# Two steps of a conversion queue behind each of the first four blocks of the last stage, instead of behind two of them

## The chip, the cores and the metric

The kernel runs on one core of a Trainium2 chip. The metric is the device time of one execution in microseconds (us). Inputs are fp32 arrays; 1.6 us (0.3%) and more can be told from no change with this kernel's spread.

## What is computed

Three layers, one behind the other, for a batch of 2, 768 positions and 512 channels (8 heads of 64). The last one, in which the change lies, is shortened here from the reference:

```python
x = attention(q, k, v, n_global, n_local)      # banded, with a bias by distance
xt = x.transpose(0, 2, 1)                      # token mixing, then channel mixing
u = x + (np.maximum(xt @ w_tok1, 0.0) @ w_tok2).transpose(0, 2, 1)
x = u + np.maximum(u @ w_ch1, 0.0) @ w_ch2
theta = x @ w_theta                            # the rotation layer
zr, zi = x * np.cos(theta), x * np.sin(theta)
y = np.einsum('ts,bsd->btd', w_tok_r, zr) + np.einsum('ts,bsd->btd', w_tok_i, zi)
u = x + y
out = u + np.maximum(u @ w_ch, 0.0)
```

## The kernel before

**Arithmetic.** Every product is made of three matmuls of split operands: a value is kept as a high and a low part, and `mm3` (L71) adds high x high, high x low and low x high. So all weights and activations have to be split before TensorE can read them.

**The conversion queue.** The weights arrive as 64-bit words in 512 KB pieces. Each piece is a job with four phases, and `tick` (L162) moves every running job one phase on, issues the loads of the next jobs (two ahead, into three raw buffers, on the queue of SP) and starts one more job. The phases are `job_scale` (two instructions on ScalarE, L120 and L121), `job_join` (two on VectorE, L126 and L129, and one on GpSimd, L130), `job_high` (one on ScalarE, L138) and `job_low` (one on VectorE, L141). A full step thus issues 3 instructions on ScalarE, 3 on VectorE and 1 on GpSimd, for four jobs. `need(job)` (L178) runs steps, one behind the other, until that job is through its four phases.

**The rotation stage.** `PhaseB.run` (L1051) goes through 12 blocks, (batch, 128 positions), numbered 0 to 11 here. The order in which a block's work is written out is the order of each engine's queue, since the scheduler is switched to manual. For block i:

- `mix(i, 0)`: 24 matmuls of `y` from the rotated values `z` and three pieces of `w_tok` (`wri`), over 256 columns;
- `rotate(i + 1)`: VectorE multiplies `x` with sine and cosine (L954), ScalarE copies the high part (L955), GpSimd subtracts for the low part (L957) and puts `x` together again (L961). `z` has two buffers;
- `turn(i + 3)`: four transposes of `x` into PSUM (`xt_..p`), split by ScalarE (L588) and VectorE (L594);
- `theta(i + 2)`: 12 matmuls of `th`, five instructions of VectorE (L923 to L931) and three of ScalarE (L934 to L936, the sines);
- `mix(i, 1)`, and in blocks 7 to 11 `last`: 24 matmuls of `v` from `u` and the four pieces of `w_ch` (`wch`). `last` calls `need(wch_job)` first (L1022), and `last_split` (L1003), called in blocks 6, 8 and 10, prepares `u` on ScalarE and VectorE (L1016, L1017);
- one step of the queue (L1069), `mix(i, 2)`, and a second step where L1071 asks for it (L1072).

`turn`, `theta` and `last` share two PSUM buffers (`wps`) in turn. In the last block of a batch VectorE also adds `y` to `x` (L995, L999). When block 0 starts, `w_tok`'s pieces 11 to 13 are in the queue's phases; the rest of `w_tok` (to piece 17) and the four pieces of `w_ch` (`wch0` to `wch3`) follow.

Of the kernel before, what the change touches and what calls it, by code (L numbers as in the profile page):

```python
# [875 lines left out]
class PhaseB:  # L876
# [174 lines left out]
    def run(self):  # L1051
        K = self.k
        n = len(self.todo)
        ends = [(b, c, half) for b in range(B) for c in (2, 0, 1) for half in ((0, 1), (2, 3))]
        ends[-1:] = [(1, 1, (2,)), (1, 1, (3,))]
        for i, (b, s) in enumerate(self.todo):
            self.mix(i, 0)
            if i + 1 < n:
                self.rotate(i + 1)
            if i + 3 < n:  # L1060
                self.turn(i + 3)
            if i + 2 < n:
                self.theta(i + 2)
            if b == 1 and s in (0, 2, 4):
                self.last_split(*ends[s][0:2])
            self.mix(i, 1)
            if b == 1 and s > 0:
                self.last(*ends[s - 1])
            K.tick()  # L1069
            self.mix(i, 2)  # L1070
            if i in (0, 2):  # L1071
                K.tick()  # L1072
        self.last_split(*ends[6][0:2])
        self.last(*ends[5])
        for j in range(6, len(ends)):
            if j in (6, 8):
                self.last_split(*ends[j + 2][0:2])
            self.last(*ends[j])
# [54 lines left out]
```

## Time and profile before

| | us |
|---|---|
| median of 3 runs | 522.35 |
| lowest, highest | 521.91, 523.35 |
| the profiled execution | 523.1 |
| its span in the trace | 521.0 |
| TensorE busy (matmuls) | 503.8 |
| VectorE, ScalarE, GpSimd busy | 302.9, 238.5, 167.5 |

All times of rows are from one profiled execution, in us from the start of its span. PE is TensorE's matmuls, PEld its weight loads, DVE VectorE, ACT ScalarE, POOL GpSimd and SP the engine that issues the DMAs. A row of a timeline holds instructions of one kind that follow each other, with their count; `[x <-y]` at its end is idle time of the engine before it and what ended that. The granted clock is a share of full speed: 1.00 is TensorE's level of 2.4 GHz, 0.50 that of 1.2 GHz. The rotation stage starts at 342 us and goes to the end; its blocks 0 to 6 take 11.6 to 11.7 us each.

### The profile page before, as it was taken

Reading aid. Unit: us, or ns where it says so; the run is one execution under the profiler, and the core shown is the slowest. Engines: PE = TensorE matmul, PEld = TensorE weight load, DVE = VectorE, ACT = ScalarE, POOL = GpSimd, SP = SyncE. Lnnn points to the kernel's source line nnn. Section 1 sums busy time; section 2 is a strip of 40 time slices with the busy share of each in tenths; the row PEclk is TensorE's granted clock in tenths of the full one; section 3 lists DMA queues with packets and bytes.
Section 4 is the critical chain, followed back from the end, with each engine's and each line's share of the span. In section 5 each row is a group of like instructions: output and inputs, shape, how many; then the busy total and the mean of one; then the engine's idle time right before and its main releaser. Section 6 shows DMA issues by size and latency. Waiting matters only on the chain.

```text
span 521.0 us, 7902 instructions
## 1 busy us (share of the span) xinstructions
PE 503.8 (97%) x2994; PEld 442.1 (85%) x2994; DVE 302.9 (58%) x676; ACT 238.5 (46%) x463; POOL 167.5 (32%) x175
## 2 busy tenths in 40 slices
PE   7999999999899999999999999999999996999997
PEld 3888878787889999998989889888888885889997
DVE  4667775269975661116473664578785864433252
ACT  4888887347765441112554535325554432133010
POOL 6645454133342320001331152235454433223000
PEclk9999999899999999999999999999999998999999
DMA  7977546135453430002442122212120000000012
GB/s 224 280 203 190 160 125 178 46 122 155 128 161 122 129 115 0 1 0 70 121 135 81 42 81 62 84 59 82 40 82 1 1 0 1 20 21 20 21 62 101
DMA packets 30620, 45.93 MB, mean 88 GB/s; under 512 B 1904, under 2 KB 22384, under 8 KB 30576
## 3 DMA queue, kind: packets, MB, share of 16 engines
q1 hardware_dynamic: 30576, 45.36, 29.0%
q8 instruction: 25, 0.41, 0.3%
q14 instruction: 19, 0.16, 0.1%
HBM read 42.21 MB, written 3.15 MB: 87 GB/s over the span
## 4 chain that ended last, share of the span: by engine, by line
PE 80%; DVE 10%; ACT 3%; DMA 2%; POOL 1%; issue 1%; POOLq 0%; SPq 0%; DVEq 0%; ACTq 0%
PE gp L77 19%; PE h L77 18%; PE y L77 17%; PE v L77 7%; PE th L77 6%; PE o L350 4%; PE t L426 3%; PE mm L77 3%; PE s L383 2%; DVE cvs L126 1%; DVE x L803 1%; POOL base L273 1%; DMA a<-v 1%; DVE cvt L129 1%; ACT e L405 1%
## 5 line engine op out<-in xcount | busy, mean ns | idle before, releaser
L130 POOL TENSOR_TENSOR cvt<-cvt,cvs 128x512 int32<-128x512 int32 (+1 forms) x57 | 76.4, 1340 | 221.2 <-DVE cvt L129 214.0
L77 PE MATMUL gp<-xh,wc 128*128 128x384 f32 x384 | 103.7, 340 | 1.9 <-DVE xl L594 1.6
L77 PE MATMUL h<-wc,g 128*128 128x512 f32 x432 | 102.5, 391 | 0.0
L77 PEld LDWEIGHTS h<-wc,g 128*128 128x128 f32 x432 | 80.6, 188 | 15.8
L590 DVE SCALAR_TENSOR_TENSOR g<-gp,g 128x384 fp32r<-128x384 f32 x48 | 26.7, 557 | 93.3 <-ACT g L588 93.1
L77 PEld LDWEIGHTS gp<-xh,wc 128*128 128x128 f32 x384 | 69.9, 188 | 3.3 <-DVE xl L594 1.8
L77 PE MATMUL gp<-xl,wc 128*128 128x384 f32 x192 | 64.6, 337 | 0.0
L588 ACT ACTIVATE g<-gp 128x384 fp32r<-128x384 f32 x48 | 23.5, 490 | 80.5 <-PE gp L77 80.5
L77 PE MATMUL y<-wri,z 128*128 128x256 f32 (+1 forms) x288 | 53.9, 342 | 0.0
L77 PE MATMUL y<-wri,s 128*128 128x256 f32 (+1 forms) x288 | 52.8, 338 | 0.0
L77 PEld LDWEIGHTS y<-wri,z 128*128 128x128 f32 x288 | 45.5, 191 | 6.9
L426 PE MATMUL t<-ident,e 128*128 128x128 f32 x176 | 48.0, 285 | 3.2 <-ACT at L433 3.1
L77 PEld LDWEIGHTS y<-wri,s 128*128 128x128 f32 x288 | 44.8, 188 | 6.7
L405 ACT ACTIVATE e<-e,mn 128x256 f32<-128x256 f32 (+1 forms) x96 | 39.3, 482 | 17.6 <-DVE mn L395 17.6
L126 DVE SCALAR_TENSOR_TENSOR cvs<-cvt,cvs 128x512 int32<-128x512 int32 (+1 forms) x57 | 43.9, 770 | 0.1
L426 PEld LDWEIGHTS t<-ident,e 128*128 128x128 f32 x176 | 31.7, 185 | 11.3 <-ACT at L433 11.0
L120 ACT ACTIVATE cvt<-raw 128x512 f32<-128x512 f32 (+1 forms) x57 | 37.4, 656 | 2.2 <-issue 2.2
L121 ACT ACTIVATE cvs<-raw 128x512 int32<-128x512 uint16 (+1 forms) x57 | 37.5, 658 | 0.0
L77 PEld LDWEIGHTS gp<-xl,wc 128*128 128x128 f32 x192 | 36.1, 188 | 0.9
L395 DVE CUSTOM_DVE_ANT_0 e<-s,base 128x256 f32<-128x256 f32 (+1 forms) x96 | 32.8, 395 | 5.5 <-PE warm L284 2.3
L934 ACT ACTIVATE w<-w 128x512 f32<-128x512 f32 x12 | 7.6, 632 | 61.1 <-DVE w L931 61.1
L350 PE MATMUL o<-v,at 128*128 128x65 f32 x192 | 32.3, 252 | 0.0
(132 smaller groups left out, 799.7 us busy)
## 6 DMA issues: line engine op xcount, KB each, us to landing
raw<-w_ch SPq DMA_DIRECT2D x28, 512.0 KB, 3.5
raw<-w_tok SPq DMA_DIRECT2D x21, 512.0 KB, 3.5
k<-k SPq DMA_DIRECT2D x8, 480.0 KB, 4.2
q<-q SPq DMA_DIRECT2D x8, 384.0 KB, 3.1
v<-v SPq DMA_DIRECT2D x8, 384.0 KB, 4.5
out<-o SPq DMA_DIRECT2D x11, 256.0 KB, 2.1
raw<-w_theta SPq DMA_DIRECT2D x4, 512.0 KB, 3.6
a<-v SPq DMA_DIRECT2D x8, 240.0 KB, 5.2
```

Of the source, the lines that this page charges most:

```text
L77: self.nc.tensor.matmul(out, lhsT=a, rhs=b, start=first and i == 0, stop=last and i == n - 1)
L120: nc.scalar.activation(out=f(t), in_=f(top), func=AF.Copy, scale=2.0**-111)
L121: nc.scalar.activation(out=s, in_=nxt, func=AF.Copy, scale=2.0**-13)
L126: nc.vector.scalar_tensor_tensor(out=s, in0=t, scalar=-(1 << 31), in1=s, op0=ALU.bitwise_and, op1=ALU.bitwise_or)
L130: nc.gpsimd.tensor_tensor(out=t, in0=t, in1=s, op=ALU.add)
L350: self.nc.tensor.matmul(po[:, j * OW : j * OW + D + 1], lhsT=at, rhs=v[:, j * (D + 1) : (j + 1) * (D + 1)], start=first, stop=last,)
L383: nc.tensor.matmul(ps[j][:, ii, c0:], lhsT=t["q"][pj, i * P : (i + 1) * P], rhs=kf[pj, i * KW - P + c0 : i * KW + P], start=True, stop=True,)
L395: nc.vector.tensor_tensor_reduce(out=e, in0=ps[j][:, ii, c0:], in1=self.base[2 * hp + j][min(i, 1)], op0=ALU.add, op1=ALU.min, scale=-SCAL ...
L405: nc.scalar.activation(out=e, in_=e, func=AF.Exp, bias=mn[:, ii, j : j + 1], scale=-1.0,)
L426: nc.tensor.transpose(pt[:, ii, c, :], e[j][:, ii, c * P : (c + 1) * P], self.ident)
L588: nc.scalar.activation(out=hi, in_=ps, func=AF.Relu if relu else AF.Copy)
L590: nc.vector.scalar_tensor_tensor(out=lo, in0=ps, scalar=0.0, in1=f(hi), op0=ALU.max, op1=ALU.subtract)
```

## The change

```diff
             K.tick()
             self.mix(i, 2)
-            if i in (0, 2):
+            if i < 4:
                 K.tick()
```

Blocks 1 and 3 get a second step of the queue each, behind `mix(i, 2)`. No job, load or instruction is added or dropped; the order of the jobs stays. By the code, the steps and the phases of `w_ch`'s pieces fall as follows:

| block | steps before | `w_ch` before | steps after | `w_ch` after |
|---|---|---|---|---|
| 0 | 2 | | 2 | |
| 1 | 1 | | 2 | |
| 2 | 2 | scale 0 | 2 | scale 0, 1; join 0 |
| 3 | 1 | scale 1; join 0 | 2 | scale 2, 3; join 1, 2; high 0, 1; low 0 |
| 4 | 1 | scale 2; join 1; high 0 | 1 | join 3; high 2; low 1 |
| 5 | 1 | scale 3; join 2; high 1; low 0 | 1 | high 3; low 2 |
| 6 | 1 | join 3; high 2; low 1 | 1 | low 3 |
| 7, `need` in `last` | 2 | high 3; low 2, 3 | 0 | |
| 7 to 11 | 1 each | (empty steps) | 1 each | (empty steps) |

## Rows read from the trace of the kernel before

**Rows 1.** Page, section 2: TensorE's busy tenths and clock, 40 slices of 13 us

```profile
PE   7999999999899999999999999999999996999997
...
PEclk9999999899999999999999999999999998999999
```

**Rows 2.** TensorE's waits, 300 to 521 us: total us, times, longest us

```profile
PE v L77 <- DVE wch L141: 3.2, 1, 3.2
PE v L77 <- ACT wch L138: 1.5, 1, 1.5
```

**Rows 3.** Timeline, TensorE, from 428: start, length, line, operation, out<-in, [idle before]

```profile
432.75 1.11 PE L77 MATMUL v<-u,wch 128*128 128x256 f32 x8
...
446.36 3.01 PE L77 MATMUL y<-wri,s 128*128 128x256 f32 x24
...
455.23 3.04 PE L77 MATMUL v<-u,wch 128*128 128x256 f32 x24
458.11 2.95 PE L77 MATMUL y<-wri,s 128*128 128x512 f32 x12
460.89 3.02 PE L77 MATMUL y<-wri,z 128*128 128x256 f32 x24
```

**Rows 4.** Stretches: length; PE, PEld, DVE, ACT, POOL busy; clock; DMA; GB/s

```profile
353.91:365.56 11.65, 11.65 (x66) 10.05 (x65) 10.10 (x13) 5.65 (x11) 6.61 (x5) 1.00 0.31 91
...
438.94:442.61 3.67, 3.67 (x16) 3.45 (x17) 0.67 (x1) 0.00 (x0) 0.00 (x0) 0.50 0.02 4
```

**Rows 5.** Timeline of VectorE in blocks 6 and 7

```profile
425.35 1.23 DVE L1017 TENSOR_TENSOR u<-x,u 128x1024 fp32r<-128x1024 f32 x1 [2.97 <-ACT u L1016]
426.49 0.69 DVE L141 SCALAR_TENSOR_TENSOR wch<-cvt,wch 128x512 fp32r<-128x512 f32 x1
427.09 0.68 DVE L126 SCALAR_TENSOR_TENSOR cvs<-cvt,cvs 128x512 int32<-128x512 int32 x1
...
428.15 2.39 DVE L954 TENSOR_TENSOR w<-x,w 128x512 f32<-128x512 f32 x2
431.81 0.69 DVE L594 TENSOR_TENSOR xt<-xt_4p,xt 128x512 fp32r<-128x512 f32 x1 [1.26 <-POOL s L957]
...
435.95 0.43 DVE L931 TENSOR_SCALAR w<-w 128x512 f32<-128x512 f32 x1
436.29 0.68 DVE L141 SCALAR_TENSOR_TENSOR wch<-cvt,wch 128x512 fp32r<-128x512 f32 x1
438.92 0.69 DVE L141 SCALAR_TENSOR_TENSOR wch<-cvt,wch 128x512 fp32r<-128x512 f32 x1 [1.95 <-ACT wch L138]
```

**Rows 6.** Timeline of ScalarE in block 7

```profile
437.67 0.71 ACT L936 ACTIVATE w<-w,halfpi 128x512 f32<-128x512 f32 x1
438.28 0.61 ACT L138 ACTIVATE wch<-cvt 128x512 fp32r<-128x512 f32 x1
```

**Rows 7.** Timeline of VectorE in blocks 0, 1 and 5

```profile
351.52 0.69 DVE L141 SCALAR_TENSOR_TENSOR wri<-cvt,wri 128x512 fp32r<-128x512 f32 x1
...
356.31 2.38 DVE L954 TENSOR_TENSOR w<-x,w 128x512 f32<-128x512 f32 x2
...
364.46 0.68 DVE L141 SCALAR_TENSOR_TENSOR wri<-cvt,wri 128x512 fp32r<-128x512 f32 x1
...
403.63 0.69 DVE L995 TENSOR_TENSOR x<-y,x 128x512 f32<-128x512 f32 x1 [0.66 <-PE y L77]
404.23 1.28 DVE L954 TENSOR_TENSOR w<-x,w 128x512 f32<-128x512 f32 x2
```

**Rows 8.** Timeline of GpSimd in block 1

```profile
358.10 3.01 POOL L957 TENSOR_TENSOR s<-w,s 128x512 fp32r<-128x512 f32 x2
```

**Rows 9.** Timeline of TensorE: where blocks 5 and 6 start

```profile
400.57 3.01 PE L77 MATMUL y<-wri,z 128*128 128x256 f32 x24
...
412.20 3.01 PE L77 MATMUL y<-wri,s 128*128 128x256 f32 x24
```

**Rows 10.** DMA issues, 335 to 521 us: count, KB, median us to landing

```profile
raw<-w_ch SPq DMA_DIRECT2D x4, 512.0 KB, 3.9
```

## Prediction

> **What bounds the kernel now.** I first read the page's slices: TensorE is busy nine tenths and more nearly everywhere in the rotation stage (342 to 521 us of the span), with one hole in the slice that begins at 430 us, and the clock row dips in that same slice [rows 1]. The waits of TensorE after 300 us then name the hole. Two waits of matmuls on `v` make up almost all of it, 3.2 us on VectorE's `wch` at L141 and 1.5 on ScalarE's `wch` at L138 [rows 2]. Everywhere else in the stage TensorE waits for nobody: in block 1 it is busy 11.65 of 11.65 us at clock 1.00 [rows 4]. So the rotation stage is TensorE's own time plus that one stall, and only the stall can be won.
>
> The stall sits in block 7, at the first call of `last`. By the code, blocks 0 to 6 run 9 steps of the queue, and the fourth piece of `w_ch` needs 11 from there to be finished; so `K.need(K.wch_job)` in block 7 issues the two missing steps back to back, just before the matmuls that read them. On VectorE the low half of `wch2` (436.29) stands behind the five instructions of theta(9), the last of them at 435.95 [rows 5]. On ScalarE the high half of `wch3` (438.28) stands behind the sines of theta(9), the last at 437.67 [rows 6]; its low half follows on VectorE at 438.92 [rows 5]. TensorE's order has nothing else to do meanwhile.
>
> **What the stall costs.** From the start of `v` in block 7 (432.75) to the start of block 8 (446.36) TensorE needs 13.61 us for 24 matmuls of `v` and 12 of `y` [rows 3]. The same two pieces in block 8 take 458.11 - 455.23 = 2.88 and 460.89 - 458.11 = 2.78, together 5.66 [rows 3]. The excess is 13.61 - 5.66 = **7.95 us**. The two waits are 4.7 of that [rows 2]. The other 3.25 are the clock: after the first wait the granted clock goes from 1.00 to 0.50 (the 1.2 GHz level) for 438.94 to 442.61 [rows 4], so the rest of `v` and the `y` behind it run slowly. If the waits go, I expect the clock loss to go with them, because TensorE holds 1.00 through the blocks before [rows 4].
>
> **The change, part by part.** It adds no instruction and no byte, and since a step issues only to ScalarE, VectorE, GpSimd and SP, TensorE's order stays as it was. Two steps move: one more behind block 1, one more behind block 3. Blocks 0 to 6 then run 11 steps, `wch3` is finished in block 6, and the `need` of block 7 finds nothing to do. *Gain*: 7.95 us if nothing else is late.
>
> *Is `wch3` in time?* Its low half is issued where block 6 now has that of `wch1`, at 426.49 [rows 5]; TensorE wants it no earlier than 432.75 [rows 3]. That leaves 6 us for VectorE to run late.
>
> *The double steps.* This is the only place where something can be paid. A rotation must deliver `z(i+1)` before block i+1 starts on TensorE, and a double step delays it on VectorE. The trace of before shows a double step only behind a block without a backlog; after the change four follow each other. From rotation(2) at 356.31 to the next step at 364.46 is 8.15 us [rows 7], the case behind a double step, with no idle time for TensorE's theta left in it. From a double step's start at 351.52 to its rotation at 356.31 is 4.79 [rows 7]. A double block thus takes VectorE about 12.94 us, against (400.57 - 353.91)/4 = 11.67 on TensorE [rows 4, 9] (353.91 is where the window of block 1 starts). The backlog grows by 1.3 us a block. Worked out: rotation(3) at 356.31 + 12.94 = 369.25, rotation(4) at 382.19, rotation(5) at 395.13. GpSimd finishes a rotation's subtractions 4.80 us after it starts on VectorE (358.10 + 3.01 = 361.11, against 356.31) [rows 7, 8], so `z(5)` is ready at 399.93. Block 5 starts at 400.57 [rows 9], and GpSimd's half is read by its third matmul, 2 x 0.12 later (2.88/24 from block 8's `v` [rows 3]): 400.81. **Margin 0.9 us**; that of `z(4)` is 1.27 larger.
>
> Then the backlog falls. Rotation(5) at 395.13 + 8.15 = 403.28 for block 4's step, a half step of low and join that takes 428.15 - 426.49 = 1.66 [rows 5], then two additions of `y` at 404.23 - 403.63 = 0.60 each [rows 7]: rotation(6) at 406.14, against 404.23 before, and `z(6)` at 410.94 for 412.20 [rows 9]. Behind that, block 5's step no longer joins (428.15 - 427.09 = 1.06 less [rows 5]), and VectorE is at most 0.85 late into block 6. Block 6 has no join either, so rotation(8) starts at about 427.9 instead of 428.15.
>
> *Bounds of the double steps.* The pair of multiplies of a rotation takes 2.38 beside a join and 1.28 alone [rows 7], so a double block can be 1.10 cheaper or, if the second join hits another such pair, 1.10 dearer. Over three blocks `z(5)` comes between 396.6 and 403.2: a price of zero to 2.4 us at block 5's start. I take zero, since the 12.94 is put together from stretches that already hold both joins and lie next to each other in the trace. Below zero is excluded: with TensorE busy all of a block, an earlier `z` shortens nothing.
>
> *The Trainium skill's rule against the change.* The page "SBUF — State Buffer", section "Who interferes with whom", says that a VectorE instruction with two SBUF inputs and a GpSimd instruction that reads SBUF exclude one another for a whole instruction, whichever issued second. The 2.38 against 1.28 agrees with it. By the rule the two joins that move in beside rotations can each block one more VectorE instruction, and `z(5)` would come at the late bound: 514.4 + 2.4 = 516.8. That mechanism is the first rival.
>
> *DMAs.* SP has no other work in blocks 0 to 6, and loads wait only for one of three raw buffers. Where it gets tightest, the load of `wch3` can start when block 2's first step has scaled `wch0`, and is read in block 3's second step, over a block (11.67 us) later; it takes 3.9 to land [rows 10]. Price 0.
>
> *What is late next in block 7.* `v` takes the PSUM buffer of `xt_4p`, which VectorE leaves at 431.81 + 0.69 = 432.50 [rows 5], only 0.25 before `v` begins. With rotation(8) at 427.9 and no join beside it this gets earlier by 0.25 to 1.35; if I am wrong on that, it costs some tenths. The operand `u` is ready at 425.35 + 1.23 = 426.58 [rows 5], six us ahead.
>
> *Sum.* The profiled execution took 523.1 us (span 521.0), which is 0.75 above the median of the runs. It would take 523.1 - 7.95 = 515.15; from the median, 522.35 - 7.95 = **514.4**, my forecast.
>
> **Rivals.**
> - *Smaller gain, the double steps bite.* `z(5)` comes after 400.81. For it: the margin is 0.9 us and is worked out over three blocks that the trace never shows in a row. Against: TensorE never waited for a `z` in before. Priced by the upper bound, 2.4 us at most; 514.4 + 2.4 = 516.8, and 520 if that wait too brought the clock loss of 3.25. Usually a few tenths to 1.5 us: 514.7 to 516.
> - *Not what it says.* The steps are done early, but `v` in block 7 then waits for another thing (the PSUM buffer, or `u`). To keep half of the 7.95 us, VectorE's low half of `xt_4p` would have to be some us later than now, while I work out that it is earlier. About 518; if all of the stall stayed, 522.35.
> - *Slower.* The stall moves to block 5's start. VectorE's double block would have to take so long that `z(5)` costs the same 7.95 and 1.6 more. With a clock loss of 3.25 in it, `z(5)` must be some 6.3 us late, so each of three double blocks (6.3 + 0.9)/3 = 2.4 us longer than 12.94; from there on the kernel is slower, at about 524. The largest single effect in the rows is 1.10.
>
> **How the numbers follow.** Forecast 0.72; smaller gain 0.18; not what it says 0.07 (0.04 of that within the bound of no change); slower 0.03. About 0.3%, 1.6 us, is what a measurement of this kernel can tell from no change. The forecast and the first rival lie beyond it: faster 0.72 + 0.18 + 0.03 = 0.93, same 0.04, slower 0.03. Below, the range goes 1.2 under the forecast: the runs of before spread over 1.4 us, and part of the excess (the clock's 3.25) need not be the same in each. Above, it goes to 517.2, the first rival's 2.4 us and a little more.
>
> **What would show it.** Right: no wait of `v` on `wch`; `v` in block 7 takes 2.88 us and the `y` behind it 2.78; clock 1.00 through block 7; the low half of `wch3` near 427; rotation(5) near 395.1 on VectorE and GpSimd done near 399.9, with block 5 still starting near 400.6. VectorE's idle time before theta should be gone in blocks 2 and 4. Wrong: a wait of `y` on GpSimd or ScalarE at the start of block 4, 5 or 6, a wait of `v` in block 7 on anything, or a clock under 1.00 anywhere between 345 and 500.

## The result and the profile after

| | before | after |
|---|---|---|
| median (us) | 522.85 (4 runs, 521.91 to 523.90) | 513.76 (4 runs, 513.52 to 514.97) |
| ratio | | 0.9838, interval 0.9818 to 0.9859 |
| the profiled execution, its span | 523.1, 521.0 | 513.82, 511.9 |
| block 0's start to block 8's start | 342.23 to 446.36: 104.13 | 341.14 to 437.33: 96.19 |
| block 8's start to the end of the span | 74.64 | 74.57 |

The kernel is faster by 1.6%. Between the starts of blocks 0 and 8 it is 104.13 - 96.19 = 7.94 us shorter, behind that it is the same. The rotation stage itself starts 1.09 us earlier (341.14 against 342.23), which the change cannot have done; where that comes from is told with the experiments. Times of after are compared with predicted ones by adding this 1.09.

The page's slices of after, which answer to [rows 1], have no hole and no dip in the rotation stage:

```profile
PE   8999999899899999999999999999999999999997
...
PEclk9999999999999999999999999999999999999999
```

From 300 us on, TensorE's waits [rows 2] are down to one that was there before:

```profile
PE gp L77 <- DVE xt L594: 0.3, 1, 0.3
```

TensorE's timeline of after (start, length, line, operation, count): block 5's start, then block 7's `v` and second half of `y`, and block 8, which answer to [rows 3, 9]:

```profile
399.49 3.01 PE L77 MATMUL y<-wri,z 128*128 128x256 f32 x24
...
431.67 3.04 PE L77 MATMUL v<-u,wch 128*128 128x256 f32 x24
434.54 2.95 PE L77 MATMUL y<-wri,z 128*128 128x512 f32 x12
437.33 3.02 PE L77 MATMUL y<-wri,s 128*128 128x256 f32 x24
```

`v` and `y` of block 7 take 437.33 - 431.67 = 5.66 us, what they take in block 8. VectorE's timeline of after, which answers to [rows 5, 7]: the rotations (L954) of 2, 3, 4 and 5, the second step behind block 3 (L141, L126), rotation(6), then the split of `u` (L1017), the low half of `wch3`, rotation(8) and the low half of `xt_4p`:

```profile
355.23 2.39 DVE L954 TENSOR_TENSOR w<-x,w 128x512 f32<-128x512 f32 x2
...
368.18 2.39 DVE L954 TENSOR_TENSOR w<-x,w 128x512 f32<-128x512 f32 x2
...
381.13 2.39 DVE L954 TENSOR_TENSOR w<-x,w 128x512 f32<-128x512 f32 x2
...
391.88 1.16 DVE L141 SCALAR_TENSOR_TENSOR wch<-cvt,wch 128x512 fp32r<-128x512 f32 x1 [0.84 <-ACT wch L138]
393.00 0.69 DVE L126 SCALAR_TENSOR_TENSOR cvs<-cvt,cvs 128x512 int32<-128x512 int32 x1
...
394.07 2.40 DVE L954 TENSOR_TENSOR w<-x,w 128x512 f32<-128x512 f32 x2
...
405.20 1.38 DVE L954 TENSOR_TENSOR w<-x,w 128x512 f32<-128x512 f32 x2
...
424.22 1.23 DVE L1017 TENSOR_TENSOR u<-x,u 128x1024 fp32r<-128x1024 f32 x1 [2.97 <-ACT u L1016]
425.36 0.68 DVE L141 SCALAR_TENSOR_TENSOR wch<-cvt,wch 128x512 fp32r<-128x512 f32 x1
425.97 1.28 DVE L954 TENSOR_TENSOR w<-x,w 128x512 f32<-128x512 f32 x2
428.44 0.69 DVE L594 TENSOR_TENSOR xt<-xt_4p,xt 128x512 fp32r<-128x512 f32 x1 [1.18 <-ACT xt L588]
```

The rotations are 12.95, 12.95 and 12.94 us apart, against 11.67 of a block on TensorE: the backlog is there, as worked out. GpSimd's timeline of after shows what it leaves: `z(5)` is ready at 395.87 + 3.01 = 398.88, and block 5's third matmul comes at 399.49 + 0.24 = 399.73, 0.85 us later.

```profile
395.87 3.01 POOL L957 TENSOR_TENSOR z<-w,z 128x512 fp32r<-128x512 f32 x2
```

### The profile page after: what moved, and what is told of

It reads as the page before. It is cut to its first block, busy times and chain, and to the rows that moved or that the text cites. A ratio compares the mean times of both kernels' runs of the same rounds, so it can differ in the third digit from the quotient of the medians.

```text
span 511.9 us, 7909 instructions
## 1 busy us (share of the span) xinstructions
PE 499.7 (98%) x2994; PEld 438.6 (86%) x2994; DVE 303.9 (59%) x676; ACT 238.9 (47%) x463; POOL 167.6 (33%) x175
## 4 chain that ended last, share of the span: by engine, by line
PE 87%; DVE 7%; ACT 3%; DMA 1%; issue 1%; DVEq 0%; ACTq 0%
PE y L77 20%; PE gp L77 19%; PE h L77 18%; PE v L77 7%; PE th L77 7%; PE o L350 5%; PE t L426 4%; PE s L383 3%; PE mm L77 3%; ACT e L405 2%; DVE x L803 1%; DVE cvs L126 1%; DVE xl L594 1%; DVE cvt L129 1%; DVE wc L141 1%
## 5 line engine op out<-in xcount | busy, mean ns | idle before, releaser
L126 DVE SCALAR_TENSOR_TENSOR cvs<-cvt,cvs 128x512 int32<-128x512 int32 (+1 forms) x57 | 44.0, 772 | 0.0
```

The source lines that it names most:

```text
L126: nc.vector.scalar_tensor_tensor(out=s, in0=t, scalar=-(1 << 31), in1=s, op0=ALU.bitwise_and, op1=ALU.bitwise_or)
```

## The experiments

**The changed kernel and the kernel before, again.** The medians differ by 9.1 us, the trace explains 7.94. The changed kernel was timed once more beside the kernels that follow, and two more executions of the kernel before were traced.

> The changed kernel once more, beside the others. Theory: the gain is the stall of block 7, 7.95 us, and the rest of the 9.1 us between the medians lies outside the rotation stage and differs from execution to execution. Then 513.5 to 514.5 us, and the span from block 8's start to the end as long as before (74.6 us). Rival: the extra 1.1 us belong to the change; then the rotation stage itself would be over 9 us shorter.

> The kernel before once more, for its parts: the executions of before lie between 520.8 and 524.0 us. Theory: the two waits in block 7 are the same in each (4.7 us, since they come from the order of VectorE and ScalarE), block 7 to block 8 takes 13.6 us within 0.5, and most of the spread comes from a clock loss at 97 to 100 us, between the attention and the token mixing, which some executions of every kernel have and others not (1.7 us). Rival: the spread comes from block 7, and the gain of the change is 7 us in some executions and 10 in others.

> The same as the run before this one, for a second draw: block 7's start to block 8's start 13.6 us within 0.5, the rest of the difference ahead of 110 us.

The changed kernel again took 513.87 us (five runs, 513.51 to 515.29; ratio 0.9834, interval 0.9814 to 0.9854), with 437.11 - 340.93 = 96.18 us from block 0 to block 8. TensorE's timeline in the first of the two further executions of before (block 7's `v`, block 8's start), and its stretch from 98 to 100 us, with columns as in [rows 4]:

```profile
432.71 1.11 PE L77 MATMUL v<-u,wch 128*128 128x256 f32 x8
...
446.62 3.01 PE L77 MATMUL y<-wri,s 128*128 128x256 f32 x24
```

```profile
98.00:100.00 2.00, 2.00 (x6) 1.52 (x6) 0.00 (x0) 0.00 (x0) 0.00 (x0) 0.50 0.80 195
```

The same rows of the second:

```profile
431.86 1.12 PE L77 MATMUL v<-u,wch 128*128 128x256 f32 x8
...
445.34 3.04 PE L77 MATMUL y<-wri,s 128*128 128x256 f32 x24
```

```profile
98.00:100.00 2.00, 2.00 (x11) 1.59 (x10) 0.00 (x0) 0.06 (x1) 0.06 (x1) 1.00 0.47 92
```

The stretch from `v` to block 8 takes 13.91 and 13.48 us, with the same waits of 3.2 and 1.5; less 5.66, the stall costs 8.25 and 7.82 in these two, 7.95 in the first. Between the attention and the token mixing TensorE stands still for over a microsecond, and behind that the clock falls to 0.50 in some executions; the traces show it in the kernel before and three others. TensorE's first matmul behind that gap and the first of the next product, in the profiled execution of before, then in that of the changed kernel:

```profile
96.51 0.73 PE L77 MATMUL mm<-xh,w 128*128 128x512 f32 x1 [1.16 <-DVE x L343]
...
110.70 4.57 PE L77 MATMUL mm<-h,w 128*128 128x512 f32 x19
```

```profile
96.90 0.48 PE L77 MATMUL mm<-xh,w 128*128 128x512 f32 x1 [1.54 <-DVE x L343]
...
109.58 5.76 PE L77 MATMUL mm<-h,w 128*128 128x512 f32 x24
```

The stretch takes 14.19 us with the loss and 12.68 without: 1.51. The mean granted clock of an execution tells the two kinds apart. With the loss, seven executions of before have a median of 523.42 and two of the changed kernel beside them 515.25: 8.2 apart. Without it, only two of before are left (521.66 and 522.66), and three of the changed kernel with a median of 513.59: 8.6 apart; eight executions of before without it, timed later, have a median of 521.93, 8.3 above the same three. So the change is worth about 8 us. The ninth between the medians depends on how many executions had the other loss, which lies 240 us ahead of what the change touches. It also explains the 1.09 us by which the rotation stage started earlier: the profiled execution of before had that loss, the one of after did not (1.51 less the 0.39 by which before came out of the gap earlier is 1.12).

**Which of the two steps matters.** The edits, each a kernel of its own:

```diff
-            if i in (0, 2):
+            if i < 3:            # e2: block 1 only
+            if i in (0, 2, 3):   # e3: block 3 only
+            if i in (0, 2, 4, 6):# e4: the same number as the change, never two blocks in a row
```

> Double steps in blocks 0, 1 and 2: ten steps before block 7, so one is left for need there, the low half of wch3. Theory: what costs is where VectorE and ScalarE stand when the missing pieces are asked for, not the number of steps. Without a join in block 6, theta(9) ends on VectorE at about 433.5 (in the time of before), the low half of wch3 at 434.2, and TensorE wants it at the 12th matmul of v, 432.75 + 11 x 0.12 = 434.1: a wait of 0.1 to 0.3, no clock loss, 513.8 to 514.4 us. Rival: each step left costs half of the stall; then about 518 us.

> Double steps in blocks 0, 2 and 3: also ten steps before block 7. Theory: as with blocks 0, 1 and 2, 513.8 to 514.4 us, since the place of the step in blocks 1 to 3 is hidden under TensorE either way. Rival: half of the stall stays, about 518 us; or one of the two places matters, and the two kernels differ by over 1 us.

> Double steps in blocks 0, 2, 4 and 6: eleven steps before block 7, as in the changed kernel, but never two double steps in a row, so no backlog on VectorE. Theory: TensorE is the bound in both, the same time as the changed kernel within 0.3 us; the only difference is that z(5) is ready over 4 us before block 5 instead of 0.9. Rival: the backlog costs something in the changed kernel that its waits do not show; then this one is faster by some tenths or more.

By the trace, block 0 to block 8 takes 439.10 - 342.65 = 96.45 us with block 1's step alone, 437.35 - 340.89 = 96.46 with block 3's alone, and 439.06 - 342.87 = 96.19 with the spread steps, as in the changed kernel. The medians (in that order 515.52, 513.84 and 515.09; ratios 0.9839, 0.9837 and 0.9842, each within 0.9816 to 0.9863) differ by how often the other clock loss fell into the five runs: the executions without it took 513.58 and 514.17, 513.58 to 513.84, and 513.47. TensorE's weight loads for `v` with block 3's step alone, and VectorE's end of theta(9) with the low half of `wch3` behind it:

```profile
432.93 1.60 PEld L77 LDWEIGHTS v<-u,wch 128*128 128x128 f32 x13 [0.24 <-DVE wch L141]
```

```profile
431.85 0.43 DVE L931 TENSOR_SCALAR w<-w 128x512 f32<-128x512 f32 x1
432.19 0.68 DVE L141 SCALAR_TENSOR_TENSOR wch<-cvt,wch 128x512 fp32r<-128x512 f32 x1
```

One step is still left for `need` there, and it costs 0.24 us, at the 12th matmul, where it was expected. So the first step moved is worth 7.7 us and the second 0.27 (96.46 - 96.19), in either place. What costs is not the number of steps but what stands in front of them, and which pieces they hold: with ten steps done, block 6 no longer has a join beside rotation(8), theta(9) leaves VectorE 2.76 us sooner (432.19 - 340.89 = 91.30 from block 0's start, against 436.29 - 342.23 = 94.06 before [rows 5]), and only one low half remains behind it, with no high half behind the sines. This reading comes from the traces; no run changes one of these alone. The backlog of four double steps in a row costs nothing: the kernel without it takes the same 96.19.

**How much room is there.** The changed kernel, with the low half of `wch0` written again and again in block 3's second step, which delays VectorE just ahead of rotation(5):

```diff
+        for _ in range(1 + again):     # 3 (e5) or 9 (e6) in block 3's second step
             self.nc.vector.scalar_tensor_tensor(
                 out=r(job["lo"]), in0=job["x"], scalar=2.0**-8, in1=job["hi"],
```

> The changed kernel, with the low half of wch0 written three times more in the second step of block 3, which keeps VectorE 3 x 0.60 = 1.8 us longer just before rotation(5). Theory: z(5) has 0.85 us to spare, so TensorE waits 0.95 us on GpSimd at block 5's start, the clock stays, and the kernel is 1.0 us slower than the changed one: about 514.8. Rival: the margin is not what decides (z is asked for later, or the backlog is taken up elsewhere): no wait, 513.8.

> The same with nine more, 9 x 0.60 = 5.4 us on VectorE before rotation(5). Theory: TensorE waits 5.4 - 0.85 = 4.55 us at block 5's start, on ScalarE and GpSimd, the clock falls as it did in block 7 of the kernel before and costs about 3 more: 513.8 + 4.55 + 3 = 521.3, close to the kernel before. This is the slower rival of the prediction at the dose where it begins. Rival: a wait of that length costs only itself: 518.3.

With three more, VectorE's and TensorE's timelines at block 5's start (one line has been added above, so L142 is L141):

```profile
391.50 3.34 DVE L142 SCALAR_TENSOR_TENSOR wch<-cvt,wch 128x512 fp32r<-128x512 f32 x4 [0.83 <-ACT wch L138]
394.76 0.68 DVE L126 SCALAR_TENSOR_TENSOR cvs<-cvt,cvs 128x512 int32<-128x512 int32 x1
```

```profile
399.12 0.40 PE L77 MATMUL y<-wri,z 128*128 128x256 f32 x2
400.65 2.88 PE L77 MATMUL y<-wri,z 128*128 128x256 f32 x22 [1.13 <-POOL z L958]
403.37 0.60 PE L622 MATMUL xt_2p<-ident,x 128*128 128x128 f32 x4
```

The step's low half holds VectorE for 394.76 - 391.50 = 3.26 us instead of 393.00 - 391.88 = 1.12: 2.14 more, not 1.8. Less the margin of 0.85 that gives 1.29; the third matmul should come at 399.12 + 0.24 = 399.36 and comes at 400.65, 1.29 later. The margin is what decides. Block 0 to block 8 takes 438.34 - 340.77 = 97.57 us, 1.38 more than the changed kernel; the median is 516.42 (ratio 0.9888, interval 0.9864 to 0.9912; the two executions without the other clock loss took 514.72 and 514.99). With nine more, the same two timelines, then stretches with columns as in [rows 4], the last of them the whole time in which the clock is down:

```profile
391.46 7.70 DVE L142 SCALAR_TENSOR_TENSOR wch<-cvt,wch 128x512 fp32r<-128x512 f32 x10 [0.84 <-ACT wch L138]
399.07 0.69 DVE L126 SCALAR_TENSOR_TENSOR cvs<-cvt,cvs 128x512 int32<-128x512 int32 x1
```

```profile
404.90 4.26 PE L77 MATMUL y<-wri,z 128*128 128x256 f32 x22 [0.91 <-POOL z L958]
409.00 0.60 PE L622 MATMUL xt_2p<-ident,x 128*128 128x128 f32 x4
```

```profile
401.00:403.00 2.00, 0.00 (x0) 0.00 (x0) 1.50 (x1) 1.00 (x2) 2.00 (x2) 0.55 0.00 0
...
401.16:408.02 6.86, 3.91 (x16) 3.62 (x17) 5.54 (x7) 1.48 (x3) 4.92 (x4) 0.50 0.00 1
```

VectorE is held 7.61 us, 6.49 more; less 0.85 that is 5.64, and the third matmul comes 5.59 late (404.90 against 387.40 + 11.67 + 0.24, with block 4's start at 387.40). The clock falls as expected, but costs 443.98 - 340.73 = 103.25, less 96.19 and less 5.59: 1.47 us. Of that 1.38 are the clock: the 22 matmuls take 409.00 - 404.90 = 4.10 us to the next transposes, against 403.37 - 400.65 = 2.72 with three more writes, where the clock held. That is less than half of the 3 expected. The stretches show why: the clock is at 0.50 already while TensorE stands still, and back at 408, so that TensorE is busy for only 3.91 of 6.86 us. In the kernel before, the same time is 6.84 us, and TensorE is busy for 5.78 of it:

```profile
437.88:444.72 6.84, 5.78 (x20) 5.09 (x21) 2.57 (x5) 1.01 (x2) 0.00 (x0) 0.50 0.03 10
```

The kernel takes 521.78 us, ratio 0.9996 (0.9981 to 1.0012): with VectorE 6.5 us later at one place, the gain of the change is gone.

**Is the clock a part of the price.** Two kernels that leave the two steps where the kernel before has them, and give TensorE something to do:

```diff
             self.mix(i, 1)
+            if i == 7:           # e7
+                self.mix(i, 2)
             if b == 1 and s > 0:
                 self.last(*ends[s - 1])
             K.tick()
-            self.mix(i, 2)
+            if i != 7:
+                self.mix(i, 2)
```

```diff
+        if (b, c, blocks[0]) == (0, 2, 0):   # e8, in last, block 7's call
+            for _ in range(24):
+                nc.tensor.matmul(v[:, 0], lhsT=r(K.wch[0][0][:, 0:P]), rhs=r(u[:, 0, 0]),
+                                 start=True, stop=True)
```

> The kernel before, but in block 7 the 12 matmuls of mix(7, 2) come ahead of v instead of behind it: TensorE has 2.78 us of its own work while the two steps of need run. Theory: the wait on wch2 shrinks to about 0.45 us, the one on wch3 stays near 1.8, and the clock does not fall: block 8 starts 5.5 us earlier than before, 516.9 us. Rival: the clock loss has nothing to do with the long wait: only the 2.8 us covered by work are gained, 519.6.

> The kernel before, with 24 extra matmuls ahead of v in block 7 (they write the first half of v, which the real ones then start over): 2.87 us of useless work that TensorE does in the stall. Theory: the clock stays at full, so although work is added, v and y behind it run at 0.12 and 0.23 us a matmul: block 8 starts about 2.5 us earlier than before, 519.9 us. Rival: without a clock loss to win back, the filling changes nothing, 522.4, or costs up to 2.9.

Block 7's `v` with mix(7, 2) ahead of it, and a stretch right behind the second wait:

```profile
436.39 0.39 PE L77 MATMUL v<-u,wch 128*128 128x256 f32 x1 [0.36 <-DVE wch L141]
438.30 3.66 PE L77 MATMUL v<-u,wch 128*128 128x256 f32 x15 [1.53 <-ACT wch L138]
441.80 3.01 PE L77 MATMUL y<-wri,s 128*128 128x256 f32 x24
```

```profile
439.00:440.00 1.00, 1.00 (x5) 0.97 (x5) 0.00 (x0) 0.00 (x0) 0.00 (x0) 0.50 0.00 0
```

And with the 24 extra matmuls (the row of L1031), with a stretch from the first wait's end to block 8, then `v` and `y` of the kernel before for comparison:

```profile
433.11 3.01 PE L1031 MATMUL v<-u,wch 128*128 128x256 f32 x24
435.95 1.11 PE L77 MATMUL v<-u,wch 128*128 128x256 f32 x8
437.40 0.38 PE L77 MATMUL v<-u,wch 128*128 128x256 f32 x1 [0.34 <-DVE wch L141]
439.31 0.51 PE L77 MATMUL v<-u,wch 128*128 128x256 f32 x2 [1.53 <-ACT wch L138]
440.04 1.81 PE L77 MATMUL v<-u,wch 128*128 128x256 f32 x13 [0.22 <-DVE wch L141]
441.69 2.94 PE L77 MATMUL y<-wri,z 128*128 128x512 f32 x12
444.47 3.00 PE L77 MATMUL y<-wri,s 128*128 128x256 f32 x24
```

```profile
437.00:444.47 7.47, 5.38 (x30) 4.39 (x29) 3.00 (x6) 2.26 (x5) 0.00 (x0) 1.00 0.10 35
```

```profile
438.94 3.86 PE L77 MATMUL v<-u,wch 128*128 128x256 f32 x15 [1.53 <-ACT wch L138]
442.61 3.92 PE L77 MATMUL y<-wri,z 128*128 128x512 f32 x12
```

The first is a miss by half. The waits shrank as expected (0.36 and 1.53), but the clock fell all the same, and 15 matmuls took 441.80 - 438.30 = 3.50 us, against 441.69 - 439.31 = 2.38 in the second kernel, where it held. Block 0 to block 8 takes 441.80 - 341.58 = 100.22 us, 3.91 less than before instead of 5.5 less, between theory and rival; the median is 518.15 (ratio 0.9918, 0.9898 to 0.9938).

In the second kernel the clock held: `y` takes 2.78 us again, and block 8 starts at 444.47 - 342.58 = 101.89 us, 2.24 less than before, with 24 matmuls more. The granted clock is 1.00 where it was 0.50 in the kernel before [rows 4], and that is how useless work can make the kernel faster: the clock's loss is part of the price of the stall. Its size can be read here as well: 15 matmuls of `v` took 442.61 - 438.94 = 3.67 us before and `y` 446.36 - 442.61 = 3.75, so the clock's part was 3.67 - 2.38 + 3.75 - 2.78 = 2.26 us.

Timed the second kernel is faster by only 0.2% (521.15; ratio 0.9979, 0.9964 to 0.9993), 0.7 us where 2.5 were expected. Its twelve executions are of several kinds. Three with a mean clock of 1.000 have a median of 520.29, against 521.59 for the 15 of before beside them without the other loss. Five at 0.997, among them the traced one, which has the other loss, have 521.11, against 523.25 for the seven of before with it. Four at 0.995 took 521.19 to 521.84; whether the clock fell in the stall there was not traced, and neither was the shortest execution of before, 520.80 at 0.997. What decides whether it falls stays open: the same 1.53 us wait has it fall in one of the two traces and not in the other.

**One step fewer.** A double step in block 0 alone (`if i == 0`).

> A double step in block 0 alone: eight steps before block 7, three left for need. Theory: what TensorE waits for is where VectorE and ScalarE get through theta(9), after which the pieces come one behind the other; a third step adds only its own length, so block 8 starts 0.9 to 1.5 us later than before, 523.5 us. Rival: each step left costs a fixed share of the stall, some 4 us: 526 to 527.

This run did not test what it was meant to: by the code, `need` for the last piece of `w_tok`, in block 5, runs the missing step already, so block 7 has two steps left, as in the kernel before. Block 0 to block 8 takes 446.19 - 341.40 = 104.79 us, with a wait of 0.7 us in block 5 on VectorE's last piece of `w_tok`; the ratio is 1.0025 (1.0006 to 1.0043).

**The other clock loss.** The changed kernel, with `self.warm_up(ps_o, 7)` at the end of the attention.

> The changed kernel, with 7 extra matmuls of zeros (512 columns) at the end of the attention, where TensorE stands still for 1.65 us at 95 to 97 us. Theory: the clock loss that some executions show right behind this gap goes away, the extra matmuls fit into the gap, and the times draw together at 513.5 to 513.9 us, about 0.2% under the changed kernel's mean. Rival: the loss comes from what TensorE did ahead of the gap, or the extra matmuls delay the next stage: the same spread of 513.5 to 515.3, or all executions some tenths later.

TensorE's timeline with the extra matmuls and the first matmul of the next stage, which came at 96.90 in the changed kernel:

```profile
95.84 1.67 PE L284 MATMUL warm<-zero 128*128 128x512 bf16 x6
98.21 0.47 PE L77 MATMUL mm<-xh,w 128*128 128x512 f32 x1 [0.69 <-ACT cvs L121]
```

The clock held in all four executions (mean 0.999 and more) and they lie within 514.63 to 515.08 us, which speaks for the gap as the cause of that loss but is too few to show it. The next stage starts 1.3 us later than in the changed kernel's trace, behind a new wait of 0.69, and the median of 514.91 is above the changed kernel's 513.87. How much of the 1.3 is due to the extra matmuls was not separated. No kernel here is faster than the changed one by more than its spread.

## Why the prediction was right

- **The gain.** Predicted 7.95 us as the excess of block 7, measured 7.94 between the two traces; 514.4 predicted, 513.76 measured, inside 513.2 to 517.2. The waits on `wch` went, and the clock loss with them. Both numbers use the same trace of before, so their agreement says that nothing else moved between blocks 0 and 8; to a hundredth it is luck, since the excess is 8.25 and 7.82 in the two other executions of before.
- **The clock, mis-sized.** That the clock is a real part of the excess is shown by the filling matmuls. But the prediction put all of the 3.25 beside the two waits down to it, and it was 2.26. The other 0.99 is there at full clock too: with the filling matmuls `v` and `y` take 444.47 - 435.95 = 8.52, less 5.66 and less the waits of 0.34 and 1.53. Of this 0.22 is a third wait, on the low half of `wch3`. The forecast did not suffer, because it took the price from the whole stretch.
- **The double steps.** 12.94 us each was the sum from two stretches of before; 12.94 to 12.95 came out. Rotation(5) was put at 395.13 and came at 394.07 + 1.09 = 395.16, `z(5)` at 399.93 and came at 399.97. The price of zero was right, and the margin of 0.9 (0.85 measured) was shown by the three-fold delay to be what decides. The smaller gain as a rival was thus a near thing: 0.85 us of 12.94 x 3.
- **The Trainium skill's rule** on VectorE and GpSimd ("SBUF — State Buffer", "Who interferes with whom") holds in the rows: a rotation's two multiplies take 2.39 beside a join and 1.28 without one. Its cost was already in the 12.94: three double steps in a row came out at that length, so the late bound of that rival did not come.
- **Blocks 6 and 7.** Too careful: VectorE was to be up to 0.85 late into block 6, and rotation(8) at 427.9. It came at 425.97 + 1.09 = 427.06: the lateness was gone when `u` was split (424.22 + 1.09 = 425.31, against 425.35 before [rows 5]). The PSUM buffer of `xt_4p` is free at 429.13 + 1.09 = 430.22 instead of 432.50, 2.3 us earlier, where 0.25 to 1.35 was worked out.
- **The slower rival** exists as a mechanism: at 6.5 us of delay the kernel is level with before. Its term that was mis-sized is the clock, taken at 3.25 and measured at 1.38 there. Nothing in the change comes near that delay.
- **The difference between the medians** was 1.1 us more than the sum. By their times, two of the four executions of before (523.35 and 523.90) had the other clock loss, and one of the four of after (514.97). The prediction took the spread of the runs into its range without knowing where it came from.

## What to carry to other kernels

A helper that "finishes what is missing" just ahead of its reader runs behind all that is queued on the helper's engines; count the steps that come before the reader, and move one into an earlier stretch where those engines are idle and their results have slack. Price a stall by the whole stretch against an undisturbed copy of it, not by its waits alone, since the clock can add about half of them again (2.26 to 4.7 us here). Where moved work leaves a queue longer than the block it is hidden in, add up the backlog over the blocks and compare it with the first deadline: here four blocks went through with 0.85 us to spare.

## What the runs showed of the hardware

- TensorE's clock went to its 1.2 GHz level behind a 3.16 us wait in each of the three executions of before that were traced, and behind waits of 0.36 and 1.53 us in one kernel but not in another with waits of 0.34 and 1.53.
- What a fall costs varies with how much TensorE has to do in it: 2.26 us where the clock was down for 6.84 us and TensorE busy for 5.78 of them, 1.38 where it was down for 6.86 and TensorE busy for 3.91.
- Behind the gap ahead of the token mixing the clock falls in some executions of a kernel and not in others. It fell behind 1.16 us in an execution of before and held behind 1.54 in one of the changed kernel, so the length of the gap alone does not decide it. The fall costs 1.51 us there, most of the 1.66 us between the two kinds of executions of the changed kernel (515.25 and 513.59).
